# A fused attention and feed-forward kernel: the clock warm-up moved to the very front, and one term of the inverse's last step moved from TensorE to VectorE

## Chip, cores and metric

The kernel runs on one core of one Trainium2 chip. The metric is the device time of one execution in microseconds (us). The core has five engines with a queue each, which run their instructions in order: TensorE (PE in the profile, its weight loads PEld), VectorE (DVE), ScalarE (ACT), GpSimd (POOL) and SyncE (SP). SP, ACT and POOL also issue DMAs.

## What is computed

The reference is Nystroem attention for 8 batches of 8 heads, 576 rows of 64, with 32 landmarks per head, followed by a feed-forward part without a nonlinear function:

```python
q_lm = q.reshape(B, H, m, S // m, D).mean(axis=3)          # m = 32, S // m = 18
k_lm = k.reshape(B, H, m, S // m, D).mean(axis=3)
A = sm(q, k_lm); Bm = sm(q_lm, k_lm); C = sm(q_lm, k)      # softmax of a b^T / 8
Z = Bm^T / (norm1(Bm) * norminf(Bm) + 1e-6)
for _ in range(6):
    Z = 2 * Z - Z @ Bm @ Z
attn = A @ Z @ C @ v                                       # to x: [4608, 512]
out = ((x @ w1) * (x @ w2)) @ w3 @ w_out
```

Inputs and output are float32. The six rounds of Z approximate the inverse of the 32 x 32 matrix Bm of each head.

## The kernel before

Four heads of one batch form a quad; there are 16 quads, two to a batch. The kernel is a list of some 1,300 small tasks, each for one engine: `add(name, engine, cost, function, deps, ...)`. The tasks' order on all engines is one list written out in the text `ORDER` (lines 39 to 116), from which `Plan.run` (line 149) takes the instructions one by one. A number behind a task's name there is the buffer or PSUM bank that it gets. The costs in `add` do not reach the chip: they are what the list was planned with. What one engine does is the list read for that engine; what it waits for are semaphores on the tasks' data.

The stages, by the letters of the tasks:

- Start. `ca` clears `ident` (L254, DVE), `cb` makes it the identity (L257, POOL), `cc` makes eight small constants from it on DVE, `minus2I` among them (L272 to L288). `zz` clears the tile `aT0` (L261, DVE). `wu0` to `wu3` are four groups of six products of these zeros, 128 x 512 each, whose results nobody reads (L263 to L270): they keep PE busy, so that its clock rises. Each waits for `zz` alone; the list has `wu0` first, `wu1` after the first mean, `wu3` after the first scores and `wu2` after the second mean.
- Weights. w3 and w_out are multiplied once to one matrix `w34`. Task `w3nJ` loads block J of w3 in four pieces (SP, block 0 half on ACT, L306), `trJ0` and `trJ1` transpose it into PSUM (DVE, L325), `whJ*` takes its high part as fp16 (ACT, L332) and `wlJ*` the rest (DVE, L340). `wfC` loads w_out in pieces of half a quarter, two on SP and two on ACT (L298); `wohC` takes the high part (ACT, L314), `wolC` the rest (DVE, L319). `mmJC` is three products (PE); eight of them, then a copy `woJ` on ACT (L359), make a block of `w34`. There are 64 `mm`.
- Quads. `lqN0` and `lqN1` load k and q of quad N (POOL, L407), `TN*` transposes them (DVE, L432). The means over 18 rows are 18 products with the identity for quads 0 and 1 (`mpN`, PE), additions on POOL for the others (`maN`, `mbN`, L440 and L447). `mkN` copies them (ACT, L466 and L468), `ltN` transposes (DVE, L474). `SN` and `AN` are the scores (PE). `smN`, `swN`, `sbN`, `seN*`, `ctN` make C (L498 to L524); `arN`, `amN`, `asN`, `aeN`, `auN`, `boN`, `anN`, `aTN` make A and Bm (L541 to L590), `asN` (L553) and `anN` (L581) on POOL.
- Inverse. Batches are taken in five groups: 0; 1 and 2; 3 and 4; 5 and 6; 7. `NI`, `btI`, `noI` make the start value of group I; then five rounds of `xI_x` (products, PE) and `yI_x` (`2 * old - product`, DVE, L726). The tile `xz` holds two 32 x 32 matrices side by side for each quad. The last round is `ZI`: for each quad and each 32 partitions a product of the two, and added to it in the same bank a product with `minus2I`, so that the bank has the round's result with its sign turned. `zoI` (DVE, L747) turns the sign by `blockneg` and spreads the result.
- Per batch: `CB` and `coB` (C v), `WB` (Z C v), `wpB` and `wqB`, then `UB**` (times w1 and w2) with copies `uo` on ACT (L791).
- Dense: `dBJC` products for a third of a batch's rows and two columns blocks (PE), `e` copies one half (ACT, L866), `f` multiplies it with the other (DVE, L872), `gI*` multiplies with `w34` (PE), `hI` copies (ACT, L886), `stI` stores (SP, L893).

All matrix products are issued at L243. `gw0` to `gw3` (POOL, L365) are small copies that hold back POOL's later loads until w_out is in. DMAs from SP and ACT use eight semaphores in turn: each waits until the one eight places earlier in the list has landed, and keeps what stands behind it on its queue waiting too.

Of the kernel before, what the change touches and what calls it, by code (L numbers as in the profile page):

```python
# [43 lines left out]
w3n2 woh6 ct0:0 mm01 w3n3.0:0 as0 woh7 w3n3.1 wol5 mm02 mk1:1 w3n3.2 wol6 lq20:2 mm03 w3n3 lq21 tr10:0.1 mm04  # L44
lq30:3 lt1 wh10 mm05 wol7 lw00 ae0 mm06 wl10 lq31 tr11:5 S1:6.7 lw10 A1:1.4 au0 wh11 w3n4.0:1 lq40:0 mm07 w3n4.1
ar1:1 w3n4.2 mm10:3 an0:0 w3n4 mm11 tr20:0.0 lq41 mm12 am1:2 wh20 lq50:1 mm13 wl11 as1 tr21:1 mm14 T20:0 wh21
w3n5.0:2 mm15 ma2:0 w3n5.1 ae1 wl20 mm16 w3n5.2 bo0:0 sm1:3 mm17 w3n5 wl21 mm20:4 tr30:5.1 lq51 mm21 mb2 au1
wh30 mm22 wo0 mm23 wl30 bo1 mm24 tr31:0 mm25 T21 wh31 w3n6.0:0 N0:1.4 w3n6.1 aT0:0 an1:1 mk2:0 mm30:2 bt0 w3n6.2
T30:1 mm26 wl31 lw11 wo1 sw1 mm31 w3n6 no0:0 ma3:0 mm32 lt2 mm27 sb1 T31 A2:5.0 tr40:3.0 lv0.0:0 mm33 lq60:2
ar2:0 wh40 mb3 mm34 tr41:1 S2:0.5 am2:5 wh41 mm35 lv0.1 se10:1 wl40 mm36 se11 wl41 mm40:6 ct1:1 as2 mm41 mk3:1  # L50
T40:0 w3n7.0:1 x0_0:3 mm37 lq61 sm2:6 wo2 ae2 ma4:0 y0_0:1 lt3 x0_1:7 au2 A3:1.4 w3n7.1 sw2 mm42 ar3:1 bo2:1
lq70:3 y0_1:2 am3:7 S3:3.1 an2:0 x0_2:4 mm43 tr50:7.1 w3n7.2 sm3:8 as3 mm44 wh50 mm45 aT1:1 wl50 lq71 ae3 mm46
w3n7 T41 mb4 wo3 mm50:7 y0_2:0 sb2 tr51:2 se20:0 x0_3:4 mm51 au3 wh51 mm52 lv0.2 aT2:2 sw3 mm47 y0_3:1 lq80:0
T50:1 mk4:0 x0_4:0 an3:1 wl51 mm53 lv0 sb3 tr60:4.0 mm54 se30:1 ma5:0 lt4 mm55 wh60 T51 bo3 lv1.0:1 A4:2.3 se21
wl60 wo4 y0_4:2 mm60:5 tr61:4 se31 lv1.1 mb5 aT3:3 S4:0.6 wh61 ar4:0 Z0:1 mm56 ct3:2 mm61 am4:9 mm62 lv1.2 sm4:1
mm63 lw01 mk5:1 wl61 mm57 lq81 ct2:3 sw4 lv1 lq90:1 mm64 wo5 zo0:0 lv2.0:2 ma6:0 mm65 sb4 lt5 se40:1 lv2.1
tr70:2.1 mm66 lv2.2 T60:0 wh70 lv2 S5:3.4 wl70 lv3.0:3 A5:7.1 lq91 sm5:2 mm70:0 lv3.1 as4 ar5:1 mm67 sw5 lv3.2
T61 mb6 mm71 ae4 tr71:2 wo6 se41 au4 lv3 C0:1.7 wh71 sb5 T70:1 se50:0 bo4 wl71 an4:0 mk6:0 mm72 co0:0.4 lv4.0:0
lv4.1 lq100:2 mm73 se51 lt6 ct4:0 ma7:0 W0:5 lv4.2 A6:6.3 am5:5 wp0:0 S6:2.1 wq0 ct5:1 U000:7.4.0.1 lv4 sm6:7
as5 mm74 uo0000 mm75 T71 lv5.0:1 mb7 ae5 mm76 ar6:0 uo0001 U001:5.7 au5 lv5.1 sw6 uo0010 mm77 uo0011 T80:0  # L60
U010:3.6 bo5 lv5.2 am6:0 wo7 U011:4.5 an5:1 uo0100 N1:7.3 T81 mk7:1 lv5 C1:0.3 sb6 aT4:4 as6 bt1 aT5:5 uo0101
lt7 uo0111 no1:0 ma8:0 se60:1 uo0110 d000:6.5 lv6.0:2 co1:1.9 ae6 lv6.1 A7:2.7 e000:0 au6 lv6.2 se61 S7:4.0 mb8
lv6 x1_0:3 lv7.0:3 T90:1 lv7.1 C2:6.1 y1_0:1 lv7.2 f000:0 lv7 sm7:4 ar7:1 lq101 mk8:0 sw7 lv8.0:0 d001:3.5
lq110:3 sb7 co2:0.5 lv8.1 d020:2.7 lq111 e001:1 lv8.2 ct6:2 se70:0 ma9:0 d010:1.6 lv8 e020:2 lt8 lv9.0:1 f001
x1_1:3 e010:0 lv9.1 f020 se71 d031:4.2 lv9.2 am7:6 lv9 d002:5.1 lq120:0 f010 d032:7.0 y1_1:2 e002:1 as7 T91
e031:2 d012:6.3 e032:0 f002:1 bo6:0 d022:5.4 mb9 f031 e012:1 x1_2:7 f032 e022:2 S8:1.2 f012 d030:6.0 y1_2:0
sm8:8 d011:5.3 e030:0 f022 ae7 x1_3:7 an6:0 f030 mk9:1 d021:6.4 y1_3:1 au7 sw8 lq121 g00:0 e021:1 ma10:0 e011:2
sb8 ct7:3 A8:7.6 se80:1 bo7 x1_4:5 lt9 f011 g30:1 ar8:0 an7:1 g01 f021 y1_4:2 A9:3.6 am8:3 h0:0 mb10 Z1:7 se81
T100:0 S9:4.5 zo1:1 g31 T101 W1:0 h3:1 sm9:9 W2:2 wp1:1 g10:7 wp2:0 as8 ar9:1 mk10:0 sw9 wq1 g11 wq2 lq130:1 ae8
sb9 T110:1 ma11:0 g20:1 se90:0 lt10 aT6:0 h1:2 U100:3.6.2.3 am9:1 se91 U101:0.2 uo1000 au8 S10:4.7 uo1011 as9  # L70
g21 uo1010 sm10:2 uo1001 U200:5.3.0.1 T111 mb11 h2:3 sw10 ae9 U210:2.0 ct8:0 bo8 C3:6.1 ct9:1 uo2001 uo2100 sb10
au9 uo2000 se100:1 an8:0 aT7:1 bo9 A10:3.2 uo2101 co3:1.5 lv10.0:2 mk11:1 lv10.1 N2:5.0 an9:1 ar10:0 lv10.2
U211:4.0 lv10 se101 bt2 U111:1.6 am10:6 ma12:0 lv11.0:3 uo2111 d200:2.3 st2.0 uo1110 no2:0 d211:7.0 lv11.1
# [12 lines left out]
lt15 wp3:1 g41 wq4 h8:1 wq3 f111 bo12 U400:0.3.0.1 h4:2 f121 U300:7.6.2.3 au13 uo4001 st4.0 U410:2.1 uo3001 st10
S15:4.3 uo4101 aT10:2 g60:6 st8.0 sm15:9 uo3000 an13:1 st4 uo4100 A14:1.7 aT11:3 bo13 st8 uo4000 sw15 an12:0 g61
sb15 ar14:1 lv13.1 se150:1 d402:2.0 se131 T151 h6:0 U401:4.1 ct13:1 e402:2 st6.0 U411:7.5 uo4011 am14:4 U301:6.2
lv13.2 uo4111 N3:1.7 f402:2 lv13 uo4010 as14 g70:5 se151 bt3 no3:0 uo4110 A15:0.4 ae14 g71 uo3011 ar15:0 uo3010
U310:3.7 am15:6 h7:3 U311:1.2 uo3101 st7.0 au14 x3_0:0 as15 uo3110 S14:4.6 st7 uo3100 d400:5.7 sm14:1 st6 ae15  # L90
d301:1.3 y3_0:1 uo3111 sw14 g50:0 e400:0 e301:1 g51 f301:0 sb14 se140:0 d321:2.5 se141 d430:1.3 e321:2 d331:4.6
h5:2 f321 e430:1 f400:1 st5.0 d420:2.0 e331:2 f430 d410:5.1 e420:0 f331 d311:7.4 f420 e410:1 d412:3.2 e311:2
d320:6.5 f311 e412:0 f410 bo14:0 d300:0.7 au15 d330:4.3 e300:2 g150:1 e330:1 f330 g180:0 e320:1 d432:4.3 f320
f300 g181 d310:6.5 g151 e310:1 e432:2 f310 d431:7.6 h15:1 f412 g140:4 h18:3 e431:1 g141 f431 f432 g130:5
d411:1.2 d401:0.7 d422:6.3 e401:0 g131 f401 e422:1 f422 d332:0.7 h13:0 d421:6.3 e411:2 e332:0 bo15 x3_1:5 e421:1
N4:1.8 C5:0.6 bt4 no4:2 y3_1:0 aT12:4 aT13:5 C6:1.5 an15:0 lv14.0:2 co5:0.7 st13.0 f411 an14:1 lv14.1 f421
lv14.2 f332 st18.0 d322:0.6 lv14 x4_0:2 e322:2 x3_2:3 lv15.0:3 y4_0:1 st18 d312:7.0 y3_2:2 f322 lv15.1 g190:2
# [65 lines left out]
def kernel(  # L163
# [19 lines left out]
    def bank(i):  # L183
        return banks[i]
# [840 lines left out]
```

## Time and profile before

| what | value |
|---|---|
| median of three runs | 273.46 us (272.3, 273.46, 298.8) |
| the profiled execution | 271.22 us, its span 269.4 us |
| granted TensorE clock, mean | 0.996 |
| PE busy | 254.5 us (94%), 3948 products |
| DVE busy | 192.6 us (72%) |
| ACT busy | 160.5 us (60%) |
| POOL busy | 132.1 us (49%) |
| DMA | 37.33 MB, mean 139 GB/s |

All times of the trace count from the start of the span. A line of the timeline has the start, the time, the engine, the source line, the operation, what it writes and reads, shapes and a count; in brackets stands the idle time of the engine before it and what ended that. Several instructions of one kind that follow each other are merged into a line. Products on PE overlap, so their busy times are longer than the steps from one to the next.

### The profile page before, as it was taken

Reading aid. Unit: us, or ns where it says so; the run is one execution under the profiler, and the core shown is the slowest. Engines: PE = TensorE matmul, PEld = TensorE weight load, DVE = VectorE, ACT = ScalarE, POOL = GpSimd, SP = SyncE. Lnnn points to the kernel's source line nnn. Section 1 sums busy time; section 2 is a strip of 40 time slices with the busy share of each in tenths; the row PEclk is TensorE's granted clock in tenths of the full one; section 3 lists DMA queues with packets and bytes.
Section 4 is the critical chain, followed back from the end, with each engine's and each line's share of the span. In section 5 each row is a group of like instructions: output and inputs, shape, how many; then the busy total and the mean of one; then the engine's idle time right before and its main releaser. Section 6 shows DMA issues by size and latency. Waiting matters only on the chain.

```text
span 269.4 us, 9569 instructions
## 1 busy us (share of the span) xinstructions
PE 254.5 (94%) x3948; PEld 167.1 (62%) x3948; DVE 192.6 (72%) x470; ACT 160.5 (60%) x414; POOL 132.1 (49%) x147
## 2 busy tenths in 40 slices
PE   0799999999999999999999999999999999999992
PEld 0444454454649965678868556968856597656852
DVE  4499999999999999899799986742863165403330
ACT  0466256474665857998656798744034973584532
POOL 4008999999999999998998151000300000000000
PEclk9999999999999999999999999999999999999998
DMA  7998999999985991279821572000555130142545
GB/s 167 286 250 174 193 230 233 245 251 216 266 198 143 208 224 15 53 201 217 179 41 45 119 178 70 19 2 0 150 155 136 23 80 0 43 100 58 120 116 138
DMA packets 22668, 37.33 MB, mean 139 GB/s; under 512 B 3552, under 2 KB 7904, under 8 KB 22624
## 3 DMA queue, kind: packets, MB, share of 16 engines
q1 hardware_dynamic: 15920, 23.80, 34.5%
q0 software_dynamic: 5696, 11.54, 24.3%
q10 hardware_dynamic: 1008, 1.38, 1.6%
q8 instruction: 31, 0.51, 0.8%
q14 instruction: 13, 0.11, 0.1%
HBM read 38.80 MB, written 9.44 MB: 179 GB/s over the span
## 4 chain that ended last, share of the span: by engine, by line
PE 68%; DMA 19%; DVE 8%; SPq 1%; ACT 1%; issue 1%; ACTq 0%; POOL 0%; DVEq 0%
PE bank L243 68%; DMA w3n<-in_moe_w_dram 12%; DMA u<-in_moe_w_out_dram 2%; DMA ab<-in_moe_w_out_dram 2%; DVE bank L325 2%; DVE w3t L340 1%; DMA out_dram<-osb 1%; DVE T L432 1%; DMA vb<-in_v_dram 1%; DVE wo L319 1%; DVE tiny L567 1%; DVE ea L541 1%; DVE tiny L498 1%; DVE tiny L547 0%; SPq L418 0%
## 5 line engine op out<-in xcount | busy, mean ns | idle before, releaser
L872 DVE TENSOR_TENSOR ab<-asb,bank 128x384 f16<-128x384 f16 x96 | 49.1, 544 | 38.1 <-ACT asb L866 30.2
L243 PE MATMUL bank<-aT,u 128*128 128x192 f16 x768 | 69.7, 246 | 0.0
L243 PE MATMUL bank<-w,ab 128*128 128x512 f16 (+1 forms) x296 | 69.3, 374 | 0.0
L243 PEld LDWEIGHTS <-u 128*128 128x128 f16 x768 | 63.7, 98 | 6.9 <-issue 0.9
L866 ACT CAST asb<-bank 128x384 f16<-128x384 f32 x96 | 44.2, 494 | 25.6 <-PE bank L243 22.7
L243 PE MATMUL bank<-wo,w3t 128*128 128x512 f16 x192 | 45.0, 379 | 0.0
L243 PEld LDWEIGHTS <-ab 128*128 128x128 f16 x296 | 27.4, 99 | 25.6 <-issue 1.5
L447 POOL TENSOR_TENSOR ls<-ls 128x128 f32<-128x128 f32 (+2 forms) x56 | 40.9, 730 | 3.7
L886 ACT ACTIVATE osb<-bank 128x512 f32<-128x512 f32 x35 | 21.2, 618 | 26.2 <-PE bank L243 20.5
L791 ACT CAST u<-bank 128x512 f16<-128x512 f32 x64 | 34.3, 632 | 3.9 <-PE bank L243 3.9
L581 POOL TENSOR_TENSOR ah<-ea,tiny 128x576 f16<-128x576 f32 x16 | 18.5, 1164 | 31.5 <-DVE aT L590 29.9
L440 POOL TENSOR_TENSOR ls<-nat 128x1152 f32<-128x1152 f16 x14 | 33.3, 2380 | 1.1 <-DMA nat<-in_q_dram 0.4
L243 PEld LDWEIGHTS <-w3t 128*128 128x128 f16 x192 | 18.0, 101 | 19.6 <-issue 0.7
L432 DVE STREAM_TRANSPOSE T<-nat 128x576 f32<-128x576 f32 x32 | 24.0, 750 | 1.7 <-DMA nat<-in_k_dram 1.7
L553 POOL TENSOR_TENSOR ea<-ea,tiny 128x608 f32<-128x608 f32 x16 | 19.4, 1215 | 7.2 <-DVE tiny L547 7.2
L243 PE MATMUL bank<-T 32*32 32x288 f16 (+1 forms) x320 | 19.0, 291 | 1.0 <-DVE T L474 0.7
L517 ACT ACTIVATE ec<-bank,tiny 128x288 f32<-128x288 f32 x32 | 16.3, 513 | 4.5 <-DVE tiny L509 4.5
L243 PE MATMUL bank<-vb,ecT 64*64 64x128 f32 x576 | 18.1, 272 | 0.0
L332 ACT ACTIVATE w3t<-bank 128x512 f16<-128x512 f32 x16 | 9.6, 597 | 13.4 <-DVE bank L325 13.1
L243 PEld LDWEIGHTS bank<-vb,ecT 64*64 64x64 f32 x576 | 16.4, 133 | 1.5 <-issue 0.4
L243 PE MATMUL bank<-w,wT 64*32 64x512 f16 x512 | 17.2, 379 | 0.1
L243 PEld LDWEIGHTS bank<-xz 32*32 32x32 f32 x768 | 12.9, 104 | 7.0 <-issue 3.3
(77 smaller groups left out, 303.1 us busy)
## 6 DMA issues: line engine op xcount, KB each, us to landing
vb<-in_v_dram SPq DMA_DIRECT2D x64, 144.0 KB, 5.4
out_dram<-osb SPq DMA_DIRECT2D x70, 128.0 KB, 2.4
nat<-in_k_dram POOLq DMA_DIRECT2D x16, 288.0 KB, 8.0
nat<-in_q_dram POOLq DMA_DIRECT2D x16, 288.0 KB, 8.9
w3n<-in_moe_w_dram SPq DMA_DIRECT2D x30, 128.0 KB, 8.4
w<-in_moe_w_dram POOLq DMA_DIRECT2D x4, 512.0 KB, 11.7
u<-in_moe_w_out_dram SPq DMA_DIRECT2D x4, 128.0 KB, 7.0
u<-in_moe_w_out_dram ACTq DMA_DIRECT2D x4, 128.0 KB, 7.2
```

The lines of the kernel that those rows point to most:

```text
L243: nc.tensor.matmul(out_, lhsT, rhs, start=start, stop=stop, **({} if pos is None else {"tile_position": pos}))
L332: nc.scalar.activation(out=w3t[at(f"w3t{j}")][:, 0, 4 * h:4 * h + 4].rearrange("p e g i -> p (e g i)"), in_=bank(at(f"w3f{j}{h}")), func=A ...
L432: nc.vector.transpose(out=Ts[at(f"T{n}")][:, GRP * t:GRP * t + GRP] .rearrange("p r l e -> p (r l e)").bitcast(FP32), in_=nats[at(f"nat{n} ...
L440: nc.gpsimd.tensor_tensor(out=l, in0=nat[:, :, 0:9, :], in1=nat[:, :, 9:18, :], op=ALU.add)
L447: nc.gpsimd.tensor_tensor(out=l[:, :, x:x + m, :], in0=l[:, :, x:x + m, :], in1=l[:, :, y:y + m, :], op=ALU.add)
L517: nc.scalar.activation(out=ecs[at(f"ec{n}")][:, hp, :], in_=two(f"pS{n}")[hp][:, 0:288], func=AXF.Exp, scale=SCALE, bias=t[:, 2 + hp:3 + h ...
L553: nc.gpsimd.tensor_tensor(out=ea, in0=ea, in1=tinies[at(f"ta{n}")][:, 0:19].unsqueeze(2).to_broadcast([128, 19, M]), op=ALU.subtract)
L581: nc.gpsimd.tensor_tensor(out=ahs[at(f"ah{n}")].rearrange("p g m r -> p g r m"), in0=eas[at(f"ea{n}")][:, 0:GRP, :].rearrange("p (g r) m - ...
L791: nc.scalar.copy(out=uu[at(f"u{b}{qd}")][:, wi, 512 * half:512 * half + 512], in_=bank(at(f"pU{b}{wi}{half}{qd}")))
L866: nc.scalar.copy(out=asb[at(f"as{b}{j}{ch}")], in_=d1_ps(b, j, ch)[0])
L872: nc.vector.tensor_mul(abts[at(f"ab{i // 2}")][:, 2 * j:2 * j + 2, CH * (i % 2):CH * (i % 2) + CH], asb[at(f"as{b}{j}{ch}")], d1_ps(b, j, ...
L886: nc.scalar.activation(out=osb[at(f"os{i}")], in_=bank(at(f"pE{i}")), func=AXF.Copy, scale=2.0 ** -12)
```

## The change

Two edits in the functions, and a new list:

- The zeros. `zz` is now the first task of DVE, and `ca` waits for it. There are five groups of zero products in place of four (30 in place of 24); each waits for the group before it, so that they are one chain. The first mean (`mp0`, `mp1`) and the first `mm` of each block wait for the last group, `wu4`; they no longer stand between other work.
- The last step. `ZI` issues the product of the two matrices alone: 64 instructions of the kernel, 128 products in the trace, are gone. Instead the fifth round `yI_4` has a second instruction on DVE, which adds `minus2I` to the first of the two matrices, in place.
- `ORDER` is a new list from beginning to end: the same tasks, with one more `wu`, in another order on every engine, with other buffers and banks.

The diff, without the list but for its beginnings:

```diff
-w3n0a.0 w3n0.0:0 ca w3n0a w3n0 lq00:0 wf0a.0 wf0s.0 lq01 wf0a wf0s lq10:1 wf1a.0 wf1s.0 wf1a wf1s lq11 wf2a.0
-wf2s.0 cb wf2a wf2s cc wf3s.0 wf3s zz T00:0 wu0:0 tr00:1.0 w3n1.0:1 wh00 wf3a.0 wl00 tr01:2 woh0 gw0 w3n1.1
-mp0:3 T01 wh01 wol0 woh1 wu1:4 mk0:0 wl01 w3n1.2 wol1 wf3a lt0 T10:1 woh2 gw1 w3n1 A0:5.6 woh3 S0:7.1 wol2 wu3:0
-sm0:0 w3n2.0:2 wol3 sw0 mm00:2 ar0:0 woh4 gw2 w3n2.1 mp1:3 sb0 T11 se00:0 wol4 w3n2.2 wu2:4 se01 am0:1 woh5 gw3
...
+w3n0a.0 w3n0.0:0 zz w3n0a w3n0 lq00:0 ca wu0:0 wf0a.0 wf0s.0 lq01 wf0a wf0s lq10:1 wf1a.0 wf1s.0 wf1a wf1s lq11
+wf2s.0 cb wf2s wu1:1 cc wf3s.0 wu2:2 wf3s tr00:3.0 wu3:4 tr01:5 wh00 T00:0 w3n1.0:1 wh01 wu4:6 wf2a.0 wl00 wl01
+woh1 gw0 w3n1.1 mp0:7 T01 woh0 wol0 mk0:0 wol1 w3n1.2 mm00:0 wf2a mm01 lt0 wf3a.0 T10:1 S0:1.2 woh2 w3n1 A0:4.3
+sm0:0 wf3a woh3 wol2 wol3 mm02 w3n2.0:2 ar0:0 sw0 mp1:6 T11 w3n2.1 woh4 mm03 woh5 am0:1 w3n2.2 mk1:1 wol4 as0
+wol5 w3n2 mm04 woh7 w3n3.0:0 sb0 lt1 gw1 woh6 gw2 wol7 A1:5.7 w3n3.1 gw3 lq20:2 ae0 mm05 wol6 w3n3.2 lq21 se00:0
...
-    for x in range(4):
-        add(f"wu{x}", "PE", 2.6 if x < 2 else 1.3, lambda x=x: warm(x), deps=["zz"], acq=[("P", f"pwu{x}", 1)], rel=[f"pwu{x}"],
-            at=("z", -5.0 + 2.0 * x), mode="full", kind="wu", n=2 * WARM)
+    for x in range(5):
+        add(f"wu{x}", "PE", 2.6 if x < 2 else 1.3, lambda x=x: warm(x), deps=[f"wu{x - 1}" if x else "zz"],
+            acq=[("P", f"pwu{x}", 1)], rel=[f"pwu{x}"], at=("z", -5.0 + 2.0 * x), mode="full", kind="wu", n=2 * WARM)
...
-    add("ca", "DVE", 0.2, const_a, at=("z", -10.0))
+    add("ca", "DVE", 0.2, const_a, deps=["zz"], at=("z", -10.0))
...
-                if c:
-                    deps.append(f"mm{j}{c - 1}")
+                deps.append(f"mm{j}{c - 1}" if c else "wu4")
...
-            add(f"mp{n}", "PE", 0.98, mean_mm(n), deps=loads + ["cc"], acq=[("P", f"pM{n}", 1)],
+            add(f"mp{n}", "PE", 0.98, mean_mm(n), deps=loads + ["cc", "wu4"], acq=[("P", f"pM{n}", 1)],
...
+            if x == 4:
+                nc.vector.tensor_tensor(out=new[:, 0:ns, 0, :], in0=new[:, 0:ns, 0, :],
+                                        in1=minus2I.unsqueeze(1).to_broadcast([128, ns, 32]), op=ALU.add)
...
-                    mm(ps[r, 32 * s:32 * s + 32], xz[r, s, 1, :], xz[r, s, 0, :],
-                       start=True, stop=False, pos=(32 * hb, 32 * hb))
-                    mm(ps[r, 32 * s:32 * s + 32], xz[r, s, 1, :], minus2I[r, :],
-                       start=False, stop=True, pos=(32 * hb, 32 * hb))
+                    mm(ps[r, 32 * s:32 * s + 32], xz[r, s, 1, :], xz[r, s, 0, :], pos=(32 * hb, 32 * hb))
```

More of the change, by code (lines that the diff above doesn't have):

```diff
@@ L45 @@
[L45 to L49, printed above, removed]
@@ L116 @@
+f721 st32 d702:7.0 e712:0 st31.0 g330:5 f712 e702:2 st31 f702 g331 g340:6 h33:3 st33.0 g341 st33 g350:1 h34:2
+st34.0 g351:3 h350:0 st34 h351 st3501 st3511 st3510 st3500
 """
@@ L808, in group_tasks @@
                 mode="32x32", kind="x", n=32 * k)
[L809 to L810 removed]
+            add(f"y{i}_{x}", "DVE", dve(128 * k) + (0.2 + 0.07 * k if x == 4 else 0.0), it_out(i, x),
+                deps=[f"x{i}_{x}", "cc"], acq=[("xz", f"xz{i}_{x + 1}", 1 if x == 4 else 2)],
                 rel=[f"xz{i}_{x}", f"pX{i}_{x}"], at=(p, 2.3 + 1.5 * x), kind="y")
             last = f"y{i}_{x}"
[L813 to L814 removed]
+        add(f"Z{i}", "PE", 0.05 + 0.12 * k, z_mm(i), deps=[last, "cc"], acq=[("P", f"pZ{i}", 1)],
+            rel=[f"xz{i}_5"], at=(p, 9.5), mode="32x32", kind="Z", n=32 * k)
         add(f"zo{i}", "DVE", dve(256 * k), z_out(i), deps=[f"Z{i}"], acq=[("zb", f"zb{i}", k)],
```

140 lines of the change are left out of this document (69 added, 71 removed).

## Prediction

> **What bounds the kernel now.** I read the page first (busy shares and the 40 slices), then the chain that ended last, then busy times by stretch, the timeline of the start, and the groups by form.
>
> ```profile
> PE 254.5 (94%) x3948; PEld 167.1 (62%) x3948; DVE 192.6 (72%) x470; ACT 160.5 (60%) x414; POOL 132.1 (49%) x147
> ...
> PE   0799999999999999999999999999999999999992
> ...
> DVE  4499999999999999899799986742863165403330
> ```
>
> The page's DVE slices fall off in the second half; PE's do not. By stretch (columns: window, its length, then busy time and count of PE, PEld, DVE, ACT and POOL, clock, DMA share, GB/s):
>
> ```profile
> 12.00:26.80 14.80, 14.40 (x116) 7.52 (x115) 14.80 (x27) 9.57 (x26) 6.04 (x11) 1.00 0.98 220
> 26.80:124.00 97.20, 96.04 (x1645) 57.65 (x1643) 93.66 (x229) 63.37 (x183) 93.32 (x98) 1.00 0.88 191
> 124.00:170.00 46.00, 46.00 (x775) 32.31 (x774) 39.23 (x93) 36.13 (x99) 27.39 (x27) 1.00 0.50 113
> 170.00:264.00 94.00, 93.89 (x1404) 67.82 (x1402) 40.43 (x97) 48.90 (x108) 2.28 (x2) 1.00 0.31 75
> ```
>
> Up to 124 us three engines are full at once: DVE 14.80 of 14.80 us and then 93.66 of 97.20, POOL 93.32, PE 96.04. After 124 us PE alone is (94 of 94 beside DVE's 40). The chain agrees: between 21.8 and 74.6 us its pieces are nearly all DVE's and DMA's, after that PE's:
>
> ```profile
> 1.68 6.30 DMA u<-in_moe_w_out_dram
> ...
> 8.00 5.79 DMA ab<-in_moe_w_out_dram
> ...
> 74.83 47.50 PE bank L243 x1049
> ```
>
> So a microsecond taken off PE counts surely only in the later part; before it, PE's work is fed by DVE, and DVE has no idle time to give. The start is the third place, because DVE and PE stood idle there:
>
> ```profile
> 3.61 0.33 POOL L257 TENSOR_SCALAR_AFFINE_SELECT ident<-ident 128x128 f32<-128x128 f32 x1
> 3.98 0.23 DVE L273 CAST ident<-ident 128x128 f16<-128x128 f32 x1 [2.97 <-POOL ident L257]
> 6.66 0.30 DVE L261 MEMSET aT<- 128x288 uint32 x1
> 7.02 2.74 PE L243 MATMUL bank<-aT 128*128 128x512 f16 x6 [7.02 <-DVE aT L261]
> 8.66 0.78 DVE L432 STREAM_TRANSPOSE T<-nat 128x576 f32<-128x576 f32 x1 [1.71 <-DMA nat<-in_k_dram]
> 9.85 1.28 ACT L332 ACT_TABLE_LOAD   x1 [9.85 <-DMA u<-in_moe_w_out_dram]
> 11.25 2.10 PE L243 MATMUL bank<-nat,ident 128*128 128x128 f16 x18 [1.50 <-DMA nat<-in_q_dram]
> 11.77 0.69 DVE L340 SCALAR_TENSOR_TENSOR w3t<-bank,w3t 128x512 f16<-128x512 f32 x1 [1.72 <-ACT w3t L332]
> 13.15 2.28 PE L243 MATMUL bank<-aT 128*128 128x512 f16 x6
> 15.82 1.09 PE L243 MATMUL bank<-T 128*128 128x320 f16 x20 [0.40 <-DVE T L474]
> 16.85 1.47 PE L243 MATMUL bank<-aT 128*128 128x512 f16 x6
> 18.94 1.17 PE L243 MATMUL bank<-nat,ident 128*128 128x128 f16 x18
> 19.94 1.46 PE L243 MATMUL bank<-aT 128*128 128x512 f16 x6
> ```
>
> The four bursts of zeros are at 7.02, 13.15, 16.85 and 19.94. The first two fall into PE's waits; the last two cost about 1.3 us each (1.46 less the overlap of the next product). Six take 2.74 us at first and 1.47 later: PE comes to its full rate between 13 and 17 us, and the 18 products of a mean go from 2.10 to 1.17.
>
> **The warm-up, moved.** The zeros go ahead of the memset of ident on DVE. That delays it by 0.30 us, hidden: the select on POOL that needs it is behind four load issues and begins only at 3.61. The chain of 30 products can begin near 1.2 us. From the rate of the first burst (2.74/6 = 0.46, upper bound) and of the last (1.46/6 = 0.24, lower bound) it ends between 8.4 and 15.0; with the release 6 to 10 us after the first product, as here, near 11 to 12.5. The first mean and the first product of w3 by w_out wait for it, and all of PE is queued behind. The mean waits for q until 11.25 in any case, so I cost this wait at 0 to 1.2, and the mean then takes 1.17 and not 2.10: about level. If the rate never rose, the chain would end at 15 and cost 2.8 there.
>
> What PE does next is set by DVE and the loads, not by the zeros. The new order puts both transposes of w3 ahead of the first of k, into the 1.71 us hole, and ACT's table load and first casts ahead of two w_out issues, so DVE's 1.72 us wait for ACT goes. Those holes are 3.4 us, of which I leave 0.9 for what DVE will still wait for k and q: up to 2.5 us of lead for DVE at 11 us. But the remaining w_out pieces on ACT's queue now stand among its casts, each waiting for an earlier piece to land before anything behind it on ACT may go. The first of them that matters waits for a piece issued at about 8.0; 5.79 us from issue to landing (row above) makes its issue 13.9 and its landing 18.8 to 19.7. The casts of that third of w_out, then the second mean's copies, then the last two casts stand in line on ACT, and DVE's subtracts wait for each. From there I count DVE's work up to the first w3 subtract of block 1, which opens the second row of products:
>
> ```profile
> 24.99 0.67 DVE L340 SCALAR_TENSOR_TENSOR w3t<-bank,w3t 128x512 f16<-128x512 f32 x1
> ```
>
> By the new order, one turn of a bank (0.87) and one transpose (0.7) more stand ahead of it, one transpose of ec (0.77) less: 0.8 us. So the start gains at best 2.5 - 0.8 = 1.7, and at worst, with the casts in line from 19.7, this subtract begins near 26.3 and the start loses 1.3. I take the nearer to the landing rows: a gain of 0.3. The two bursts of 1.3 us thus free PE for work that is not there yet. SP's queue keeps its order of loads, with the two last w_out pairs asked for earlier than ACT's; on POOL the first subtract of a maximum now goes ahead of three gates, 1.2 us in front of the next q and k loads, but the loads that open the gates land near 20 us anyway; I cost both at nothing, and 1.2 us of POOL if that cover is gone.
>
> **The last step, split.** Columns: line, engine, operation, tiles, shape, count; busy, mean ns.
>
> ```profile
> L243 PE MATMUL bank<-xz 32*32 32x32 f32 x128 | 3.2, 198 | 0.0
> L243 PE MATMUL bank<-minus2I,xz 32*32 32x32 f32 x128 | 3.2, 191 | 0.0
> ...
> L709 DVE TENSOR_TENSOR xz<-bank,tiny 128x128 f32<-128x128 f32 x3 | 0.8, 280 | 0.0
> ...
> L709 DVE TENSOR_TENSOR xz<-bank,tiny 128x64 f32<-128x64 f32 x2 | 0.4, 214 | 0.0
> ```
>
> ```profile
> 59.66 0.24 PE L243 MATMUL bank<-xz 32*32 32x32 f32 x5
> ...
> 60.11 0.39 PE L243 MATMUL bank<-wo,w3t 128*128 128x512 f16 x1
> ```
>
> The 128 products overlap four deep, so their 3.2 us are not their price: the whole step of one batch takes 60.11 - 59.66 = 0.45 us of PE, half of it 0.22, and for two batches at most 0.45. Of the five groups the first (59.66) stands where DVE leads: 0. The second also, by the stretch where DVE and POOL are full. The last three, in PE's part, give 0.45 + 0.45 + 0.22 = 1.1. Bounds 0 and 1.8.
>
> DVE gets five additions, 0.21 for one batch and 0.28 for two. Three stand in PE's part and are covered by dense products; two (0.5 us) stand where DVE is full. Each reads two tiles in SBUF, and such an instruction can be held by POOL:
>
> ```profile
> 19.86 0.65 DVE L319 SCALAR_TENSOR_TENSOR wo<-ab,wo 128x512 f16<-128x512 f32 x1
> 20.00 0.56 POOL L365 COPY gates<-ab 128x1 f32<-128x1 f32 x1 [4.07 <-DMA w3n<-in_moe_w_dram]
> 21.29 1.21 POOL L553 TENSOR_TENSOR ea<-ea,tiny 128x608 f32<-128x608 f32 x1 [0.73 <-DVE tiny L547]
> 21.81 1.23 DVE L319 SCALAR_TENSOR_TENSOR wo<-ab,wo 128x512 f16<-128x512 f32 x1
> ...
> L440 POOL TENSOR_TENSOR ls<-nat 128x1152 f32<-128x1152 f16 x14 | 33.3, 2380 | 1.1 <-DMA nat<-in_q_dram 0.4
> ```
>
> The same subtract takes 0.65 us alone and 1.23 when it begins inside POOL's addition: it seems to run only once that ends at 22.50. The small copy on POOL took 0.56 until the subtract before it was done. So each addition waits 0 to 2.38 us (POOL's longest), and by the nearest row 0.58. I take 0.58 for the two early groups: with the operation 1.65 us of DVE; bounds 0.5 and 5.3, passed on in full. The Trainium skill (SBUF — State Buffer, "SBUF: two separate sides") states this as an exclusive lock between VectorE with two SBUF inputs and GpSimd, in which the loser fully blocks; the trace agrees (1.23 against 0.65). It speaks against this half of the change.
>
> **The sum.** -0.3 (start) - 1.1 (products) + 1.65 (additions) = +0.25 us. The profiled execution took 271.2 (span 269.4), so 271.5 there. Two of the three runs shown are 272.3 and 273.46, 1.1 and 2.2 above it; with the lower offset 272.6. I give 272.0, between. The list that orders all instructions is new from end to end, and its effect beyond the start I cannot price: either sign, some 2 us.
>
> **Rivals.**
> - PE bounds from the start, 20%. Then the zeros' 2.6 us and all of the products' 1.8 come off, and the start by its best 1.7: -6.1 + 0.5 = -5.6, 266.4. For it: PE's 94%, and busy slices from end to end. Against it: DVE's 14.80 of 14.80. The Trainium skill (Trainium Kernel Development and Optimization, "Performance Expectations") calls matmul busy time a bad metric and weight loads' busy share a good one; here that is 62%, and in the full stretch 57.65 of 97.2, so by that page PE would have room and this rival falls. The trace gives no more than that.
> - POOL holds the additions, 10%; slower. POOL is inside some instruction for 93.32 of 97.20 us; if the three groups before 150 us each wait the full 2.38 and the chain to the first dense products hangs on them, that is 7.1 + 0.8 in place of 1.65: 278. It decides from 1.9 us a piece on.
> - The zeros don't do what they are there for, 10%: they end at 11 and PE's gaps between 14 and 25 us, where it now waits for w_out, lower the clock again. The real work there, 24 products of 0.24, a mean of 1.17 and two times 1.09 (row at 15.82), is 9 us; at half rate 18, in a window of 15 after the first mean: 3 us late, 275. Against it: the 1.50 us pause at 9.76 did not keep the clock from rising.
>
> **Chances.** The first case 60%, its own range 269 to 275. Against the median of 273.46, 2% is 5.5 us, about what a measurement of this kernel can tell from no change: below 268.0 or above 278.9. Faster is the first rival, 20%. Slower is half of the second rival, whose 278 lies close under the bound, and 3% of what the new list may do: 8%. Within 2% is the rest, 72%. The range that holds 8 in 10 reaches to the first rival and near the second: 266.4 to 277.5.
>
> **What would show it.** The profile after should have DVE full from 12 to 124 us again; the first w3 subtract of block 1 at 24 to 26.3 us; five additions of 0.2 to 0.3 us, those before 150 us longer where POOL is busy; and the PE rows of the last step without minus2I, half as long. I am wrong if that subtract (now 24.99) moves ahead by over 2 us and the end follows it, or if DVE has idle time before 100 us.

## The result

The changed kernel is slower: 275.13 us (median of 20 runs) against 272.26 us for the kernel before (20 runs), a ratio of 1.0096 with a 95% interval of 1.0078 to 1.0114. Ratios, here and below, are estimated from the runs outside a slower state of the chip and are not the quotient of the medians (1.0105 here). The profiled execution took 274.13 us, its span 272.4 us. The prediction had 272.0 us, and its sum +0.25 us against the profiled execution of before; measured is +2.9 us there, and +2.6 us by the ratio.

### The profile page after: what moved, and what is told of

The parts are those of the page before. It is cut to its first block, busy times and chain, and to the rows that moved or that the text cites. A ratio compares the mean times of both kernels' runs of the same rounds, so it can differ in the third digit from the quotient of the medians.

```text
span 272.4 us, 9336 instructions
## 1 busy us (share of the span) xinstructions
PE 255.6 (94%) x3826; PEld 166.9 (61%) x3826; DVE 198.0 (73%) x475; ACT 161.6 (59%) x414; POOL 132.5 (49%) x147
## 4 chain that ended last, share of the span: by engine, by line
PE 67%; DMA 21%; DVE 5%; SPq 3%; ACT 2%; issue 1%; DVEq 0%; ACTq 0%
PE bank L243 67%; DMA w3n<-in_moe_w_dram 13%; DMA vb<-in_v_dram 4%; DMA u<-in_moe_w_out_dram 3%; SPq L417 2%; DMA ab<-in_moe_w_out_dram 2%; ACT u L790 1%; DVE bank L325 1%; DVE wo L319 1%; DVE tiny L566 1%; DVE T L431 0%; DVE w3t L340 0%; SPq L892 0%; DVE tiny L497 0%; DVE ea L540 0%
## 5 line engine op out<-in xcount | busy, mean ns | idle before, releaser
L865 ACT CAST asb<-bank 128x384 f16<-128x384 f32 x96 | 44.4, 485 | 26.8 <-PE bank L243 21.7
L243 PE MATMUL bank<-wo,w3t 128*128 128x512 f16 x192 | 46.9, 385 | 5.7 <-DVE wo L319 2.4
L580 POOL TENSOR_TENSOR ah<-ea,tiny 128x576 f16<-128x576 f32 x16 | 18.7, 1169 | 28.3 <-DVE aT L589 26.3
L552 POOL TENSOR_TENSOR ea<-ea,tiny 128x608 f32<-128x608 f32 x16 | 19.7, 1235 | 19.9 <-DMA w3n<-in_moe_w_dram 11.0
L243 PE MATMUL bank<-vb,ecT 64*64 64x128 f32 x576 | 18.9, 272 | 0.3 <-DMA vb<-in_v_dram 0.3
L243 PE MATMUL bank<-xz 32*32 32x64 f32 (+1 forms) x768 | 15.2, 213 | 2.1 <-DVE xz L730 1.7
## 6 DMA issues: line engine op xcount, KB each, us to landing
w<-in_moe_w_dram POOLq DMA_DIRECT2D x4, 512.0 KB, 12.5
```

The source lines that it names most:

```text
L243: nc.tensor.matmul(out_, lhsT, rhs, start=start, stop=stop, **({} if pos is None else {"tile_position": pos}))
L552: nc.gpsimd.tensor_tensor(out=ea, in0=ea, in1=tinies[at(f"ta{n}")][:, 0:19].unsqueeze(2).to_broadcast([128, 19, M]), op=ALU.subtract)
L580: nc.gpsimd.tensor_tensor(out=ahs[at(f"ah{n}")].rearrange("p g m r -> p g r m"), in0=eas[at(f"ea{n}")][:, 0:GRP, :].rearrange("p (g r) m - ...
L865: nc.scalar.copy(out=asb[at(f"as{b}{j}{ch}")], in_=d1_ps(b, j, ch)[0])
```

## The profile after

First the page's busy shares and slices, then the busy times by stretch (columns as in the prediction):

```profile
PE 255.6 (94%) x3826; PEld 166.9 (61%) x3826; DVE 198.0 (73%) x475; ACT 161.6 (59%) x414; POOL 132.5 (49%) x147
...
PE   8776999978999999999999999999999999999992
...
DVE  4679999999999999999999986754655055312230
```

```profile
12.00:26.80 14.80, 9.51 (x65) 4.42 (x65) 12.30 (x23) 7.78 (x23) 5.68 (x11) 0.88 0.97 206
26.80:124.00 97.20, 93.11 (x1542) 55.56 (x1541) 94.85 (x222) 62.47 (x178) 90.84 (x94) 1.00 0.89 190
```

The 122 fewer products (128 gone, 6 zeros more) are there, and PE's first slice went from 0 to 8: the zeros start at 1.23 us. But between 12 and 26.8 us DVE, which had no idle time before, now works 12.30 of 14.80 us, and PE 9.51 where it was 14.40. After 124 us PE is full as before. So time was lost early. DVE's part of the timeline shows what it waited for:

```profile
12.63 1.29 DVE L319 SCALAR_TENSOR_TENSOR wo<-u,wo 128x512 f16<-128x512 f32 x2 [1.89 <-ACT wo L314]
...
16.51 0.69 DVE L319 SCALAR_TENSOR_TENSOR wo<-u,wo 128x512 f16<-128x512 f32 x1 [0.64 <-ACT wo L314]
...
18.22 0.69 DVE L319 SCALAR_TENSOR_TENSOR wo<-u,wo 128x512 f16<-128x512 f32 x1 [1.01 <-ACT wo L314]
```

Each time a subtract of w_out waits for its cast on ACT. ACT's part shows why the casts are late:

```profile
7.31 1.19 ACT L332 ACTIVATE w3t<-bank 128x512 f16<-128x512 f32 x2 [0.96 <-DVE bank L325]
10.95 0.32 ACTq L298 DMA_DIRECT2D ab<-in_moe_w_out_dram  x1
11.45 1.15 ACT L314 ACTIVATE wo<-u 128x512 f16<-128x512 f32 x2 [2.95 <-DMA u<-in_moe_w_out_dram]
...
13.77 1.95 ACTq L298 DMA_DIRECT2D ab<-in_moe_w_out_dram  x2
15.85 0.63 ACT L314 ACTIVATE wo<-u 128x512 f16<-128x512 f32 x1 [2.32 <-DMA w3n<-in_moe_w_dram]
17.19 0.32 ACTq L298 DMA_DIRECT2D ab<-in_moe_w_out_dram  x1
17.56 0.63 ACT L314 ACTIVATE wo<-u 128x512 f16<-128x512 f32 x1 [1.08 <-DMA w3n<-in_moe_w_dram]
18.93 1.15 ACT L314 ACTIVATE wo<-ab 128x512 f16<-128x512 f32 x2 [0.74 <-DMA w3n<-in_moe_w_dram]
...
21.66 1.15 ACT L314 ACTIVATE wo<-ab 128x512 f16<-128x512 f32 x2 [0.65 <-DMA ab<-in_moe_w_out_dram]
```

Lines marked ACTq are DMA issues on ACT's queue. A cast of a tile that is long there (`u`, at 15.85 and 17.56) stands behind an issue that waits for a landing, and the bracket names a w3 load that the cast itself does not read. The chain that ended last runs through the last issue (columns: start, time, what):

```profile
11.14 6.03 DMA w3n<-in_moe_w_dram
17.17 0.02 issue
17.19 4.45 DMA ab<-in_moe_w_out_dram
21.64 0.03 DVEq L319
21.67 1.23 DVE wo L319
```

A piece of block 1's w3, landing at 17.17, lets ACT issue the last piece of w_out; that lands at 21.64, and the last two casts of w_out can go (21.66). The chain then puts the subtract at 21.67 behind this landing, but it does not read that piece: it is the second of the pair at 20.95, began at 21.54, as soon as DVE was free, and took 1.70 us beside a subtraction on POOL:

```profile
20.95 2.30 DVE L319 SCALAR_TENSOR_TENSOR wo<-ab,wo 128x512 f16<-128x512 f32 x2
21.12 1.58 POOL L552 TENSOR_TENSOR ea<-ea,tiny 128x608 f32<-128x608 f32 x1 [10.97 <-DMA w3n<-in_moe_w_dram]
```

The same subtract took 1.23 us in before. The first w3 subtract of block 1 comes 1.65 us later than before (24.99):

```profile
26.64 0.66 DVE L340 SCALAR_TENSOR_TENSOR w3t<-bank,w3t 128x512 f16<-128x512 f32 x1
```

The second place is the first group's addition. From the timeline, DVE, POOL and PE:

```profile
56.32 2.38 POOL L439 TENSOR_TENSOR ls<-nat 128x1152 f32<-128x1152 f16 x1
...
57.89 3.23 DVE L730 TENSOR_TENSOR xz<-xz,minus2I 128x64 f32<-128x64 f32 x1
58.65 1.16 POOL L580 TENSOR_TENSOR ah<-ea,tiny 128x576 f16<-128x576 f32 x1
59.76 3.13 POOL L446 TENSOR_TENSOR ls<-ls 128x512 f32<-128x512 f32 x4
...
61.17 0.33 PE L243 MATMUL bank<-xz 32*32 32x32 f32 x16 [1.73 <-DVE xz L730]
...
62.51 0.60 ACT L332 ACTIVATE w3t<-bank 128x512 f16<-128x512 f32 x1 [3.61 <-DVE bank L325]
```

An operation of 0.23 us (group 4, POOL idle) took 3.23 while POOL ran three instructions without a pause (the third, the first of the four at 59.76, ends at 61.02, the addition at 61.12); PE waited 1.73 us for it and ACT 3.61 for the transpose behind it. The other four took 0.23 to 0.55 us.

## The experiments

There are two theories of the loss. Start (S in the expectations, and A for its cause): the new list makes the casts of w_out late, by ACT's load issues. Hold (L): POOL holds the addition, and that reaches the end. The list in between (M; its effect was not priced in the prediction) is the rest. Ratios are against the kernel before, run on the same chip, with the 95% interval; not all experiments ran on one chip. In several of these kernels the text of the list is up to two lines shorter, so that a source line's number is up to two lower than in after.

**One half of the change at a time, on the list of before.**

```diff
+            if x == 4:
+                nc.vector.tensor_tensor(out=new[:, 0:ns, 0, :], in0=new[:, 0:ns, 0, :],
+                                        in1=minus2I.unsqueeze(1).to_broadcast([128, ns, 32]), op=ALU.add)
```

> The kernel before with the last step of the change alone, under the old list: 128 products less, the addition on DVE. Theory L: the first addition begins near 58.9 us inside POOL's 2.4 us mean and is held 0.6 to 3 us; slower by 0.5 to 2.5 us, ratio 1.002 to 1.009. If products on PE are what counts, 1.1 us faster, ratio 0.996.

Measured: 1.0012 (0.9986 to 1.0038). The first two groups' additions took 0.64 and 1.89 us there:

```profile
59.56 0.64 DVE L731 TENSOR_TENSOR xz<-xz,minus2I 128x64 f32<-128x64 f32 x1
...
101.86 1.89 DVE L731 TENSOR_TENSOR xz<-xz,minus2I 128x128 f32<-128x128 f32 x1
```

```diff
-w3n0a.0 w3n0.0:0 ca w3n0a w3n0 ...
+w3n0a.0 w3n0.0:0 zz ca wu0:0 ... wu3 wu4 ...        (one chain of 30 zeros, the rest as before)
```

> The kernel before with the zeros alone moved: first on DVE, 30 products in one chain ahead of all else on PE; DVE, ACT, POOL and SP otherwise in the old order. DVE's queue does not get shorter by more than the 0.30 us that it no longer spends between its constants and the first transpose, where it waits anyway. Theory D (DVE feeds PE in the first half): the first w3 subtract of block 1 stays at 25.0 us and the time is the same, ratio 0.998 to 1.002. If PE bounds, the two bursts of 1.3 us come off, ratio 0.990. If PE's longer waits let the clock fall, 1.002 to 1.01.

Measured: 1.0009 (0.9985 to 1.0034). PE ran at half clock for two thirds of this stretch (mean 0.65). In this one execution block 1's first w3 subtract came at 26.63 and not at 25.0 us, but the twelve runs show no price:

```profile
12.00:26.80 14.80, 9.97 (x72) 5.57 (x70) 13.46 (x25) 9.39 (x27) 4.43 (x9) 0.65 0.94 212
```

On the old list neither half costs or gains anything that can be told from zero, each to about 0.25%. The loss comes with the new list.

**The new list by halves.** One kernel takes the old list up to `mm15` and the new one from there, the other the new list up to `mm15` and then the old one with the old last step.

> The changed kernel with the old list up to task mm15 (about 30 us, the zeros in four groups at their old places), then the new list for all that is left; the last step stays changed. Theory S (the new list's start costs about 2 us): first w3 subtract of block 1 back to 25 to 25.7 us, the end 1.5 to 2 us earlier than the changed kernel, ratio 1.001 to 1.004. Theory M (the new list loses in the middle, after 60 us): no gain, ratio 1.008 to 1.010.

> The kernel before with the new list up to task mm15, zeros first in one chain, then the old list; the last step as before, with its products. Theory S: 1.5 to 2 us slower than before, ratio 1.005 to 1.008, and the lateness at mm15 is kept to the end. Theory M: the same as before, ratio 0.998 to 1.002.

Measured: old start, new rest 1.0112 (1.0075 to 1.0148); new start, old rest 1.0056 (1.0034 to 1.0079). The new start alone loses half a per cent: block 1's first w3 subtract was at 27.46 us there, 2.47 late, and 1.6 us of that stayed to the end. But the old start does not mend the new list: spliced lists are lists of their own, and the two losses add up to more than the whole. So the list's two suspects were taken singly.

**The last four w_out loads.** They are moved to SP, each beside its partner, ahead of block 1's w3; casts and all else stay.

```diff
-for x, e, eng, a0 in (("s", "SP", nc.sync, 0), ("a", "ACT", nc.scalar, 2)):
+for x, e, eng, a0 in (("s", "SP", nc.sync, 0), ("a", "ACT", nc.scalar, 2) if c < 4 else ("a", "SP", nc.sync, 2)):
...
-wf2s.0 cb wf2s wu1:1 cc wf3s.0 wu2:2 wf3s ... wu4:6 wf2a.0 wl00 ... mm00:0 wf2a mm01 lt0 wf3a.0 ... sm0:0 wf3a
+wf2s.0 wf2a.0 cb wf2s wf2a wu1:1 cc wf3s.0 wf3a.0 wu2:2 wf3s wf3a ...
```

> The changed kernel with the last four w_out loads of ACT's queue issued by SP, beside their partners, so that no cast on ACT stands behind a load that waits. Theory A (that is what makes the start late): the casts of w_out 2 and 3 come 1 to 2 us earlier, the first w3 subtract of block 1 near 25 us instead of 26.6, the end 1 to 1.7 us earlier, ratio 1.003 to 1.006. If instead the order on DVE (a turn and a transpose put ahead of that subtract) is what counts, the casts come earlier and the end does not move, ratio 1.009.

Measured: 0.9997 (0.9966 to 1.0027); run again later, 1.0003 (0.9979 to 1.0027). The loss of 0.96% is gone. ACT's casts in the second run:

```profile
13.64 1.17 ACT L312 ACTIVATE wo<-u 128x512 f16<-128x512 f32 x2
16.50 1.15 ACT L312 ACTIVATE wo<-ab 128x512 f16<-128x512 f32 x2 [1.69 <-DMA ab<-in_moe_w_out_dram]
...
18.86 1.17 ACT L312 ACTIVATE wo<-ab 128x512 f16<-128x512 f32 x2
```

And by stretch:

```profile
12.00:26.80 14.80, 11.74 (x107) 5.79 (x105) 14.36 (x27) 8.20 (x22) 7.11 (x12) 1.00 1.00 228
```

The first pair of `u`, at 11.45 in after, comes at 9.59 in this run. ACT's further casts come earlier by 2.2 us (the second pair of `u`, from 15.85), 2.4 us (`ab`, from 18.93) and 2.8 us (from 21.66), and DVE is nearly full again (14.36 of 14.80), although q landed 1.5 us later in this execution than in after's (first mean at 11.53 against 10.07). Block 1's first w3 subtract is at 24.47, 2.17 us ahead of after's; the lead is still 2.17 us in block 2's first product (31.61 against 33.78) and 2.0 us in the span (270.4 against 272.4). In the first run q came as early as in after (first mean at 9.96), and the lead was 3.74 us at that subtract and 3.85 us at the last products; the ratios stand for 2.5 us. The same edit on the kernel before, as a control:

> The kernel before with the same four loads moved from ACT to SP and nothing else. ACT's table load moves from 9.85 to near 5.1 us, the first casts and DVE's first subtract from 11.77 to near 10.7. If DVE's queue sets the first half, the end comes up to 1 us earlier, ratio 0.996 to 0.999; if the loads of w_out and w3 do, no change, ratio 1.000.

Measured: 0.9966 (0.9943 to 0.9989), a third of that. In before, ACT issued two of the four at 8.00, ahead of any cast. Where this third comes from was not found: in the one trace the w3 subtract is at 25.18, not earlier.

**Queue or place?** The move changed the queue and the place in the list together. Two kernels take them apart: the early place with ACT's queue, and after's late place with SP's.

> The list of after with the last four w_out loads at the place they have in the run with all of them on SP (beside their partners, ahead of block 1's w3 loads), but still issued by ScalarE; all additions. With these loads on SP it was 0.9997 and 1.0003, after itself is 1.0096. Theory that the place in the list is what costs (a late place means a late landing of w_out's second half): 0.998 to 1.003. Theory that ScalarE's queue is what costs (its casts of w3 stand behind issues that wait for landings until some 11 us): 1.005 to 1.012, with the first casts of w3 at 11 us and not at 7.3.

> The list of after, unchanged, with the last four w_out loads issued by SP at their late places among block 1's w3 loads; all additions. Theory that the place costs: 1.006 to 1.011, with the last subtracts of w_out on VectorE as late as in after (20.95 and 23.50 us). Theory that ScalarE's queue costs: 0.998 to 1.003, with the subtracts near 18.8 and 21.3 us.

Measured: early on ACT 1.0202 (1.0183 to 1.0222), slower than both theories gave; late on SP 1.0048 (1.0024 to 1.0072), between them. Early on ACT all casts stand behind the issues, those of w3 too; the table load, which comes ahead of them all, starts at 13.43 and not at 5.06:

```profile
8.64 4.75 ACTq L296 DMA_DIRECT2D ab<-in_moe_w_out_dram  x4
13.43 1.28 ACT L330 ACT_TABLE_LOAD   x1 [13.43 <-DMA u<-in_moe_w_out_dram]
14.72 1.08 ACT L330 ACTIVATE w3t<-bank 128x512 f16<-128x512 f32 x2
```

Late on SP nothing waits behind an issue, but w_out's second half still lands late:

```profile
13.64 1.15 ACT L314 ACTIVATE wo<-u 128x512 f16<-128x512 f32 x2 [0.46 <-DMA u<-in_moe_w_out_dram]
20.10 1.15 ACT L314 ACTIVATE wo<-ab 128x512 f16<-128x512 f32 x2 [5.31 <-DMA ab<-in_moe_w_out_dram]
```

Neither theory alone holds. Step by step from after, the change of queue brings about half of the 0.9% (1.0096 to 1.0048) and the early place on SP the other half (1.0048 to 1.0003), each to within some 0.3%. But the two do not simply add up: taken the other way round, the early place on ACT's queue first costs 1.1% (1.0096 to 1.0202), and the change of queue then brings 2.0%. The early place pays only on the queue of an engine that has no casts.

**The addition.** First the whole last step undone on the kernel after, then the addition kept with one input in SBUF in place of two.

```diff
-            if x == 4:
-                nc.vector.tensor_tensor(... in1=minus2I ..., op=ALU.add)
...
+                    mm(ps[r, 32 * s:32 * s + 32], xz[r, s, 1, :], minus2I[r, :],
+                       start=False, stop=True, pos=(32 * hb, 32 * hb))
```

> The changed kernel with the last step as before: 128 products again, no addition on DVE; its list of tasks is unchanged. Theory L (an addition is held by POOL: 3.23 us for the first, against 0.23 where POOL is idle, and the end follows): about 2.5 us faster than the changed kernel, ratio to the kernel before 1.000 to 1.003. Theory S (the loss is made in the first 27 us and kept): no gain, and up to 1.1 us more for the products, ratio 1.009 to 1.013.

Measured: 1.0084 (1.0055 to 1.0113), 0.1% below after, which can't be told from none. It lies far from theory L and just under the range of theory S, and it looked as if the hold were given back later; the runs below show that this was a difference of two terms.

```diff
-                nc.vector.tensor_tensor(out=new[:, 0:ns, 0, :], in0=new[:, 0:ns, 0, :], in1=minus2I..., op=ALU.add)
+                nc.vector.tensor_scalar(out=new[:, 0:ns, 0, :], in0=new[:, 0:ns, 0, :], scalar1=0.0, scalar2=None, op0=ALU.add)
```

> The changed kernel, but the added instruction on DVE adds zero and so reads one tile of SBUF and not two; the minus 2 I is left out, so the inverse is another. Everything else is as in the changed kernel. Theory L: the instruction takes 0.2 to 0.3 us in all five groups, DVE's 3.23 us at 58 us become 0.25, and the end comes 2 to 3 us earlier, ratio 0.999 to 1.002. Theory S: the instruction is short, but the end stays, ratio 1.008 to 1.010.

Measured: 1.0112 (1.0069 to 1.0155). The edit did not take the hold away, so the run tells nothing about its price:

```profile
59.71 3.19 DVE L730 TENSOR_SCALAR xz<-xz 128x64 f32<-128x64 f32 x1
```

Then the products back on the list with the loads on SP:

> The list of after with the last four w_out loads issued by SP, and the last step of the iteration with its 128 products, as before. Compared with the run that had the same loads on SP and the addition (0.9997 of the kernel before). Theory that the addition's hold is a cost that reaches the end: the first group's hold of 3.23 us goes away and the 128 products come back at about 1.1 us, so 0.5 to 2.1 us faster than that run, a ratio of 0.992 to 0.998. Rival, that what the hold costs is given back behind 112 us because TensorE has other work by then: 0.998 to 1.003.

Measured: 0.9951 (0.9924 to 0.9977), by 0.5% below the same list with the additions: the hold reaches the end. It is also level with 0.9966, the old list with the same loads: apart from these loads, what the new order gains can't be told from zero. And the one held addition alone taken away, with the loads on SP and with the kernel after's own loads:

```diff
-            if x == 4:
+            if x == 4 and i > 0:
...
-                    mm(ps[r, 32 * s:32 * s + 32], xz[r, s, 1, :], xz[r, s, 0, :], pos=(32 * hb, 32 * hb))
+                    mm(ps[r, 32 * s:32 * s + 32], xz[r, s, 1, :], xz[r, s, 0, :],
+                       start=True, stop=i > 0, pos=(32 * hb, 32 * hb))
+                    if i == 0:
+                        mm(ps[r, 32 * s:32 * s + 32], xz[r, s, 1, :], minus2I[r, :],
+                           start=False, stop=True, pos=(32 * hb, 32 * hb))
```

> The list of after with the last four w_out loads issued by SP, the last step of group 0 with its products (16 of the 128) and that of groups 1 to 4 with the addition. Theory that the one held addition, 3.23 us for group 0, is all that the additions cost: the ratio of the run with all products back, 0.995, within 0.002, and 0.003 to 0.006 below the run with all additions. Rival, that all five additions cost, VectorE being full up to 124 us: 0.997 to 1.000. Other rival, that the hold goes to the next instruction that meets the pool engine's run: an L728 or L723 of over 2 us in the trace, and 0.998 to 1.001.

> The list of after with the last four w_out loads issued by SP and all additions, beside the run with the products for group 0 alone on the same chip. If the held addition reaches the end with 1.2 us, as the two traces from alike starts say, this run is 0.003 to 0.006 above that one, at 0.998 to 1.001 of the kernel before. If it is given back, both are within 0.002.

> The kernel after, its w_out loads on ScalarE, with the last step of group 0 by its 16 products and the addition for groups 1 to 4 alone. Theory that the held addition of group 0 costs the same on this list as with the loads on SP (1.0% there) and is most of what the change lost: 0.998 to 1.002. Theory that the load issues are nearly all of the loss and that the hold is given back here, as the run with all products back (1.0084) seemed to say: 1.005 to 1.009, since that run gave up the four later groups' saving of 0.5% as well.

Measured: 0.9901 (0.9874 to 0.9929), its partner on the same chip 1.0003 as told above, and 1.0033 (0.9998 to 1.0067). Both lie outside what the theories gave. 0.9901 is 1.0% and not 0.5% below its partner, and below the kernel with all products: the four later additions pay, which no theory had counted, and that had hidden half of the hold's price. 1.0033 lies between the two theories: the hold and the loads each cost. In the 0.9901 kernel the same stretch of the timeline has POOL's long addition, and DVE working beside it on things that read PSUM or write to it, with no hold and no wait of its own:

```profile
54.26 2.38 POOL L437 TENSOR_TENSOR ls<-nat 128x1152 f32<-128x1152 f16 x1
...
55.54 0.25 DVE L723 SCALAR_TENSOR_TENSOR xz<-xz,bank 128x128 f32<-128x128 f32 x1
...
55.72 0.81 DVE L495 TENSOR_REDUCE tiny<-bank 128x1 f32<-128x288 f32 x2
...
56.45 0.71 DVE L323 STREAM_TRANSPOSE bank<-w3n 128x512 f32<-128x512 f32 x1
56.59 1.16 POOL L578 TENSOR_TENSOR ah<-ea,tiny 128x576 f16<-128x576 f32 x1
```

The six kernels with the new list make a table:

| last step | w_out loads late, on ACT | early, on SP |
|---|---|---|
| products for all groups | 1.0084 | 0.9951 |
| products for group 0, additions for 1 to 4 | 1.0033 | 0.9901 |
| additions for all groups | 1.0096 (after) | 0.9997, 1.0003 |

Down a column: additions for the four later groups gain 0.5% (1.4 us) in both; the held one costs 0.6% (1.7 us) in after's column and 1.0% (2.8 us) in the other, each difference known to about 0.4% (1.1 us). Across: the loads cost 0.9 to 1.3%. The traces of the right column agree, since the three began their first scores within 0.2 us of each other (14.11, 14.32 and 14.21 us): their spans are 268.8, 267.5 and 270.4 us, 1.3 us for the four additions and 2.9 us for the held one. The kernel with both drawbacks taken away, 270.04 us against 272.77, beats before and after.

**The zeros.** On the old list with the loads on SP, the chain of zeros added:

> The kernel before with the last four w_out loads issued by SP (0.9966 of the kernel before by itself), and the zeros first and in one chain of 30, the rest of the list as before. Theory that the chain by itself is worth nothing and that its place in the new list matters only through ACT's loads: 0.995 to 0.999. Rival, that the chain starts the means earlier and ScalarE, no longer held by load issues, hands this on to the iteration: 0.990 to 0.994, with the first subtract of block 1's w3 before 24 us. Other rival, that the clock falls in the gaps behind the means: 1.000 to 1.006.

Measured: 0.9961 (0.9937 to 0.9985), beside 0.9966 without the chain, as the first theory said: the chain alone is worth nothing here either. And in the kernel after, the last six zeros moved into PE's gap between `mm04` and `A1`, because the clock fell to half there:

```profile
19.66:23.07 3.41, 0.91 (x3) 0.14 (x2) 3.41 (x5) 2.76 (x9) 1.95 (x2) 1.00 1.04 224
23.07:26.48 3.41, 2.86 (x9) 1.30 (x10) 3.41 (x9) 1.47 (x4) 3.41 (x9) 0.50 0.61 103
```

> The kernel after with one tile of six zeros moved from the start into the gap of TensorE between the first mm product group and block 1's first product. Theory that the clock at half from 23.07 to 26.48 us is a cost of its own: the clock stays up there, at most 0.6 us off the first w3 subtract of block 1, a ratio of 1.007 to 1.009. Theory that the products there wait for ScalarE's casts behind the load issues and that the clock only fills time that is waited anyway: 1.0090 to 1.0110, whether the clock stays up or not.

Measured: 1.0088 (1.0056 to 1.0120). The clock stayed up from 16 us on, but it was at half from about 12.0 to 15.4 us in its place, so the run does not separate the two theories by itself. Two things speak for the second. DVE, which hands PE its work there, was busy in all of both windows above (3.41 of 3.41 us), so slow products did not keep it waiting. And the kernel with the loads on SP kept its full clock (1.00 in the row above), but its lead over after is 2.17 us at DVE's w3 subtract and the same behind the half-clock stretch, at block 2's first product. That the slow products only filled time that PE would have waited is argued from this, not measured alone.

## Why the prediction was wrong, by its own steps

The time lies inside the wide range (266.4 to 277.5) and just above the first case's own (269 to 275), but 272.0 was put below the 273.46 us of the kernel before, and the change came out slower. By the terms of the sum, the run with all products back has the new list, the zeros and the old last step: 1.0084, which is +2.3 us where the sum had -0.3. The last step on that list is the rest, 1.0084 to 1.0096: +0.3 us where the sum had -1.1 + 1.65 = +0.55. So the start, with the list behind it, is the term that failed.

- What bounds the kernel: right, and it names where the loss is. DVE has no slack up to 124 us; the 2.17 us that the loads cost at DVE's w3 subtract were 2.0 us at the end.
- The start, "a gain of 0.3": this step failed. The text saw the mechanism, issues among ACT's casts that wait for an earlier landing, and put its worst case at a loss of 1.3 us with the subtract near 26.3; it came at 26.64, 1.65 late, outside the bound. It then took 0.3, near the middle of its bounds, and counted only the wait for one landing (18.8 to 19.7). The last issue came at 17.19, because it waited for a w3 load of SP's queue, landed at 21.64, and the casts of the quarters that had long landed waited as well. The loads by themselves are 0.9%, 2.5 us. The other side of the bound, up to 1.7 us from holes that the new order closes, is not seen: with the loads on SP the new list is at 0.9951 and the old one at 0.9966, both with the old last step.
- The chain of zeros: right in its price. It ended at 10.2 us (11 to 12.5 was forecast), the mean took 1.17, and the move alone was worth nothing on either loading of the old list.
- The products, -1.1: right as far as it can be told. The four later groups gain 1.4 us, known to 1.1, with their additions' own cost taken off. (The reading that the products overlap "four deep" is too low: 128 of 198 ns in 3.2 us of busy time are eight deep. The term was taken from the step of 0.45 us and does not hang on it.)
- The additions, +1.65: near at the end, by luck. Two waits of 0.58 were taken, on groups 0 and 1; it was one of 3.0 on group 0 (0.3 or less on each of the others). The bound of 2.38 for a wait, POOL's longest instruction, was too low: POOL went into its next instruction twice while the addition waited (58.65 and 59.76). At the end it was 1.7 us, and 2.8 with the loads repaired. The Trainium skill (SBUF — State Buffer, "SBUF: two separate sides") gives the lock to whichever starts first, for the whole instruction; the trace agrees as to the blocking, but not as to the order: here the addition, begun at 57.89, waited for three of POOL's instructions, two of which began after it.
- Rival PE bounds from the start: it fell. The zeros were out of the way by 10.2 us, and PE then waited, 5.3 of 14.80 us.
- Rival POOL: its mechanism was there for one group of three, with a wait above the 1.9 us from which it was to decide; the price was 1.7 us, a part of the loss and not the 278 us.
- Rival clock, 275 us: the time is near, the cause is not. The clock did fall, but no run shows a price for it.
- SP's and POOL's order "at nothing": for POOL it was not tested; its next load of k began 1.0 us later than before (23.46 against 22.45). For the loads it failed as told: the wait of an issue for the load eight places earlier joins SP's queue and ACT's.
- "DVE has idle time before 100 us" was named as what would prove it wrong, and is what the profile shows (2.5 us in 14.8).

Open: why the old start in front of the new list (1.0112) is no better than after. Its addition took 3.00 us as well, which is about 0.6 to 1.0%. Its trace points to the seam for the rest: the two w3 subtracts of block 1 come 1.32 us later than in before (26.31 and 30.56), but the first of block 2 comes 3.66 us later (34.78 against 31.12). The old start reaches block 1's second subtract late (27.92 in after), and the new list puts over 4 us of other work between it and block 2's first, where before had 1.88. No run tests this.

## What to carry to other kernels

A load issue on an engine that computes is an instruction that can wait: find what its semaphore waits for, and count every cast behind it, not only the one that reads its data. When a change brings a new order, price the first place where the bounding engine runs dry, by the latest of the landings. Two edits of opposite sign on one step (here the first group's addition and the four others) look like none until one of them is undone alone: the best kernel keeps the part that pays.

## What the runs showed of the hardware

- An addition on DVE with one SBUF input and a constant was held like that with two: 3.19 us against 3.23, 0.20 us when free. The Trainium skill (SBUF — State Buffer, "SBUF: two separate sides") names two forms that contend with GpSimd, two SBUF inputs and a mode that uses two ports; the run agrees if this form is of the second kind, which the trace does not show.
- When a held instruction gets in between two of POOL's is not settled. In after the addition got in behind the third: the second and the third began 0.05 us before the one ahead had ended, the fourth 0.08 us after. On the old list it ran when POOL's 2.37 us instruction ended (0.64 us in all), and POOL's next began 0.08 us after that end. But the subtract that was held from 21.54 got in at about 22.7 us, ahead of a small copy on POOL that had begun at 22.65 and took 0.64 us.
- The clock fell to 0.50 for 3.41 us after 3.41 us in which PE had been busy for 0.91, though its longest pause was 1.70 us. The Trainium skill (TensorE: Matmul & The Clock Gate, Part 1) counts such windows; here a window that was not fully idle was enough. With the half clock lasting some 10 us of the first 25, the two kernels with the chain on the old list lost nothing that can be told from zero (1.0009, and 0.9961 beside 0.9966).
- The start varies by itself: the two executions with the loads on SP began their first scores at 12.64 and 14.21 us, and the difference of 1.6 us was still 1.85 us at the end of their last products (263.62 and 265.47). A single trace is to be compared with that in mind.
